# Attention and two MLPs on one core: decoding the float64 weights of the first batch in fewer, wider operations

## Chip, core and metric

The kernel runs on one NeuronCore of a Trainium2 chip. The metric is the device time of one execution in microseconds, as a median over runs.

## What is computed

A two-step attention (32 packed queries read the sequence, then the sequence reads the packed result), and two MLPs on all 4608 tokens:

```python
def sm_attn(qq, kk, vv):
    s = scale * np.matmul(qq, kk.transpose(0, 1, 3, 2))
    s = s - np.max(s, axis=-1, keepdims=True)
    a = np.exp(s)
    a = a / (np.sum(a, axis=-1, keepdims=True) + 1e-09)
    return np.matmul(a, vv)
p_packed = sm_attn(p, k, v)
out = sm_attn(q, p_packed, p_packed)
x = out.transpose(0, 2, 1, 3).reshape(4608, 512)
g = x @ w_gate
x = (g / (1 + np.exp(-g)) * (x @ w_val)) @ w_out
h = x @ w_in
return (h * np.cos(h)) @ w_out2
```

Batch 8, heads 8, sequence 576, head width 64; the first MLP has 1536 hidden columns, the second 2048. q, k, v and p are float32. The weights of both MLPs come as float64: the core reads each as two 32-bit words and makes float32 of the high word.

## The kernel before

All instructions are issued in the order in which the program is written (`tc.manual_schedule`); each engine runs its own in that order, and waits on semaphores for the others. A tile's buffer comes from a pool of a tag: `w` (24 tiles of 4 KB a partition), `c` (19), `m` (12), `s` (6), and 8 PSUM banks.

**A unit** is one decode of 512 words of a partition. `u_load` has SP load the raw words (`raw_words`, L80). `u_act` runs `decode_a` on ACT: L89 takes the high word as a float, absolute value times 65536, into `dec`, and L90 makes the low exponent bits from a byte into the result. `u_dve` runs `decode_b` on DVE: L96 raises `dec` to a least value, L97 shifts it and ors it in, L100 ors in the sign. There are 24 units for the gate and value weights (`wg`, two for each block f of 128 hidden columns) and 12 for `w_out` (`wof`, o0 to o11, three for each output block o). After a unit of `w_out`, `flush_wo` splits it: ACT copies the high half into `wo` (L77), POOL subtracts for the low half (L78); it is called in `u_dve` behind the decode of the next unit, so a split stands behind that decode. `w2_decode` uses the same decode for 256 words at a time, in batches 1 to 6.

**Stages.** Batch 0 begins with `a_s1(0)` (scores of p and k, maxima, exponentials), `a_t`, `a_pp`, `a_ppt`, `a_s2(0)` (scores of q, transposes, softmax, `af`), with first units between them (L489 to L500). Then, for every batch b:

- `a_up(b)` has 12 turns f. In batch 0 a turn makes `wp` of block f+1 (`a_wp0`: PE multiplies the packed result by `wg`, ACT copies it to `wpf`), then the gate and value products of f in four PSUM banks (L357). For each half c of the sequence ACT applies silu, the pending split of the last `h` is issued (`flush_split`: L77 on ACT, L78 on DVE), DVE multiplies `h` (L381), and `extra` issues a unit: twice a turn for f below 9, then once.
- `a_down(b)` has 8 turns n: turn n multiplies `g` with `wo` of block n // 2 (L423, 36 matmuls, three for each f; f // 4 picks the unit), and ACT evicts. `steps` holds what is issued ahead of each turn: the stages of batch b+1 (`a_s1` at 0, `a_t` at 2, `a_pp` at 3, `a_ppt` at 4, `a_s2` at 5, `a_wp` at 6), and in batch 0 two units at each of 0 to 3, one at 4, and `flush_wo` at the head of 5.

A second phase (L531 on) runs the second MLP.

Of the kernel before, what the change touches and what calls it, by code (L numbers as in the profile page):

```python
# [34 lines left out]
PASSES = ((0, 0), (0, 1), (1, 0))  # L35
LEAST = float(np.array((896 + 128) << 20, np.uint32).view(np.float32))


@with_exitstack
def attention_mlp_kernel(ctx: ExitStack, tc: tile.TileContext, qT, kT, vP, pP, wgv, w1o, w2, out):  # L40
# [92 lines left out]
    def a_s1(b):  # L133
        sp = [[bank([128, HS], "s1") for _ in range(2)] for _ in range(2)]
        for h in range(2):
            for c in range(4):
# [7 lines left out]
        for r in range(2):
# [3 lines left out]
            nm = st.tile([128, 1], F32, tag="nm", name="nm")  # L148
            DVE.tensor_scalar(out=nm, in0=mx[:, 0:1], scalar1=mx[:, 1:2], scalar2=-0.125, op0=ALU.max, op1=ALU.mult)
            e = ct([128, SPAD], F32, "E")  # L150
            nc.gpsimd.memset(e[:, S:SPAD], 0.0)
            sm = st.tile([128, 2], F32, tag="sm", name="sm")
# [5 lines left out]
            z = st.tile([128, 1], F32, tag="rs", name="rs")
            DVE.tensor_scalar(out=z, in0=sm[:, 0:1], scalar1=sm[:, 1:2], scalar2=1e-9, op0=ALU.add, op1=ALU.add)
            DVE.reciprocal(out=z, in_=z)  # L160
            E[r], rs[r] = e, z
        for j in range(NPAIR):
            del kt[b, j]
# [302 lines left out]

    with tc.manual_schedule():
        load_k(0, 0)
        load_k(0, 1)
        load_p(0)  # L470
        load_k(0, 2)
        load_k(0, 3)
        for j in range(NPAIR):
            load_v(0, j)
        u_step(0, 3)
        for j in range(NPAIR):
            load_q(0, j)
        u_step(0, 5)
        DVE.memset(zero, 0.0)
# [173 lines left out]
```

## Time and profile before

| | |
|---|---|
| median of 3 runs | 1566.46 us (1564.9 to 1567.13) |
| the profiled execution | 1567.96 us, its span 1566.2 us |
| busy PE, DVE, ACT, POOL | 1538.2 (98%), 1013.9 (65%), 713.6 (46%), 19.3 us |
| mean granted clock of TensorE | 0.992 of full speed |

The rows below come from two views. The timeline of an engine gives start and length in us, engine, line of the kernel, operation, output<-input, partitions x elements and type, how many in a row, and in brackets the idle time before with what ended it. The table of stretches gives, for each stretch of us, the busy time of each engine with its number of instructions, then the granted TensorE clock as a share of full speed (PEclk), the DMA engines' busy share and GB/s. Starts are counted from the start of the span; ends of matmuls are modelled.

### The profile page before, as it was taken

The page shows a single profiled execution, that of the slowest core. Times are in us where ns is not written, and L with a number is a line of the kernel's source. Part 1 is how long each engine was busy: PE and PEld are TensorE (multiplying, and loading weights), DVE is VectorE, ACT ScalarE, POOL GpSimd, SP SyncE. Part 2 cuts the span into 40 slices and gives each one's busy share as a digit, 9 for nine tenths or more (in the row PEclk, how much of TensorE's full clock was granted, in tenths as well). Part 3 has the DMA queues.
Part 4 walks back from the last instruction along what each step waited for, and adds up shares of the span by engine and source line. Part 5 has one row for each costly group of instructions (what it writes and reads, how often), then busy time and mean ns, then how long its engine had stood idle before and what let it go on. Part 6 is the DMA issues. An engine that isn't in the chain of part 4 may idle for free.

```text
span 1566.2 us, 24858 instructions
## 1 busy us (share of the span) xinstructions
PE 1538.2 (98%) x9796; PEld 1318.5 (84%) x9796; DVE 1013.9 (65%) x1976; ACT 713.6 (46%) x1454; POOL 19.3 (1%) x34
## 2 busy tenths in 40 slices
PE   6989999999999999999999999999999999999998
PEld 4668898989899898999978888888888888888887
DVE  6986837375583737354487676766667676776765
ACT  5874726355362635334454343333433333333333
POOL 0022000000000000000000000000000000000000
PEclk8999999999999999999999999999999999999999
DMA  8542423324151432220330101010010101010000
GB/s 305 186 146 89 146 87 125 121 78 156 46 167 59 126 119 71 89 87 5 121 94 1 54 1 54 0 55 1 12 43 1 54 0 55 0 54 1 27 1 27
DMA packets 63046, 112.25 MB, mean 72 GB/s; under 512 B 6992, under 2 KB 24656, under 8 KB 62928
## 3 DMA queue, kind: packets, MB, share of 16 engines
q1 hardware_dynamic: 53712, 101.21, 19.6%
q10 hardware_dynamic: 9216, 9.44, 1.7%
q8 instruction: 77, 1.26, 0.3%
q14 instruction: 41, 0.34, 0.1%
HBM read 83.36 MB, written 27.26 MB: 71 GB/s over the span
## 4 chain that ended last, share of the span: by engine, by line
PE 95%; DVE 3%; ACT 1%; issue 0%; DMA 0%; DVEq 0%; ACTq 0%; SPq 0%
PE acc L567 25%; PE h L540 25%; PE o L423 19%; PE pg L372 9%; PE pv L372 9%; PE wp L323 3%; PE pg L357 1%; PE pv L357 1%; PE pp L184 1%; DVE wof L100 1%; PE s L208 1%; PE wp L309 1%; PE s L138 1%; PE tp L173 0%; PE wm L482 0%; DVE wof L97 0%
## 5 line engine op out<-in xcount | busy, mean ns | idle before, releaser
L567 PE MATMUL acc<-wb,g 128*128 128x512 f32 x1728 | 416.4, 390 | 3.1 <-DVE g L78 2.5
L540 PE MATMUL h<-x,wb 128*128 128x512 f32 x1728 | 415.5, 389 | 0.0
L567 PEld LDWEIGHTS acc<-wb,g 128*128 128x128 f32 x1728 | 324.6, 188 | 71.8 <-DVE g L78 3.4
L540 PEld LDWEIGHTS h<-x,wb 128*128 128x128 f32 x1728 | 324.9, 188 | 67.6
L423 PEld LDWEIGHTS o<-g,wo 128*128 128x128 f32 x2304 | 307.3, 188 | 20.2 <-issue 10.9
L423 PE MATMUL o<-g,wo 128*128 128x288 f32 x2304 | 318.1, 297 | 4.9 <-POOL wo L78 4.1
L559 ACT ACTIVATE t<-t,half_pi 128x512 f32<-128x512 f32 x144 | 104.4, 725 | 272.6 <-DVE t L557 272.6
L552 ACT ACTIVATE t<-h,quarter 128x512 f32<-128x512 f32 x144 | 99.2, 689 | 197.8 <-PE h L540 197.7
L554 DVE TENSOR_SCALAR kk<-t 128x512 f32<-128x512 f32 x144 | 61.5, 427 | 192.4 <-ACT t L552 192.4
L372 PEld LDWEIGHTS pg<-a,wp 128*128 128x128 f32 x1008 | 142.1, 188 | 29.3 <-issue 18.4
L372 PE MATMUL pg<-a,wp 128*128 128x288 f32 x1008 | 164.9, 299 | 0.0
L372 PE MATMUL pv<-a,wp 128*128 128x288 f32 x1008 | 160.7, 294 | 0.0
L372 PEld LDWEIGHTS pv<-a,wp 128*128 128x128 f32 x1008 | 143.0, 188 | 0.0
L78 DVE TENSOR_TENSOR g<-h,g 128x288 fp32r<-128x288 f32 x192 | 87.2, 454 | 51.7 <-ACT g L77 51.7
L560 DVE TENSOR_TENSOR t<-t,h 128x512 f32<-128x512 f32 x144 | 99.1, 689 | 28.2 <-ACT t L559 28.2
L378 ACT ACTIVATE silu<-pg 128x288 f32<-128x288 f32 x192 | 78.9, 411 | 72.2 <-PE pg L372 62.2
L556 DVE SCALAR_TENSOR_TENSOR t<-kk,t 128x512 f32<-128x512 f32 x144 | 99.7, 693 | 4.9
L555 DVE SCALAR_TENSOR_TENSOR t<-kk,h 128x512 f32<-128x512 f32 x144 | 99.2, 689 | 5.0
L78 DVE TENSOR_TENSOR g<-t,g 128x512 fp32r<-128x512 f32 x144 | 98.6, 685 | 0.7 <-ACT g L77 0.7
L77 ACT ACTIVATE g<-h 128x288 fp32r<-128x288 f32 x192 | 84.5, 440 | 16.4 <-DVE h L381 15.2
L77 ACT ACTIVATE g<-t 128x512 fp32r<-128x512 f32 x144 | 89.6, 622 | 0.8 <-DVE t L560 0.8
L428 ACT ACTIVATE x2e<-o 128x288 f32<-128x288 f32 x64 | 26.2, 409 | 134.6 <-PE o L423 134.6
(82 smaller groups left out, 1128.9 us busy)
## 6 DMA issues: line engine op xcount, KB each, us to landing
raw<-in_w SPq DMA_DIRECT2D x64, 256.0 KB, 2.8
raw<-in_wgv SPq DMA_DIRECT2D x24, 512.0 KB, 7.9
vt<-in_vP SPq DMA_DIRECT2D x32, 320.0 KB, 4.6
kt<-in_kT SPq DMA_DIRECT2D x32, 288.0 KB, 4.4
qt<-in_qT SPq DMA_DIRECT2D x32, 288.0 KB, 6.2
x2d<-x2e ACTq DMA_DIRECT2D x64, 144.0 KB, 1.7
x2r<-x2d SPq DMA_DIRECT2D x36, 256.0 KB, 3.8
out<-oe SPq DMA_DIRECT2D x35, 256.0 KB, 2.0
```

The lines of the kernel that those rows point to most:

```text
L77: ACT.activation(out=hi, in_=src, func=AF.Copy)
L78: eng.tensor_tensor(out=lo, in0=src, in1=hi.bitcast(F32), op=ALU.subtract)
L372: PE.matmul(out=p_, lhsT=w[u][:, x, o:o + 128], rhs=a2[u][:, y, sl], start=(n == 0), stop=(n == 5),)
L378: ACT.activation(out=s_, in_=pg, func=AF.Silu)
L423: PE.matmul(out=acc, lhsT=wo[o, f // 4][:, x, f % 4, :], rhs=g[f][:, y, sl], start=(f == 0 and i == 0), stop=(f == NF1 - 1 and i == 2),)
L540: PE.matmul(out=p_, lhsT=wb["i", f][:, x, 128 * k:128 * k + 128], rhs=x2[t][k][:, y, :], start=(n == 0), stop=(n == 11),)
L552: ACT.activation(out=t_, in_=h_, func=AF.Identity, scale=1.0 / TWO_PI, bias=quarter)
L555: DVE.scalar_tensor_tensor(out=t_, in0=k_, scalar=-C_HI, in1=h_, op0=ALU.mult, op1=ALU.add)
L556: DVE.scalar_tensor_tensor(out=t_, in0=k_, scalar=-C_LO, in1=t_, op0=ALU.mult, op1=ALU.add)
L559: ACT.activation(out=t_, in_=t_, func=AF.Sin, bias=half_pi)
L560: DVE.tensor_tensor(out=t_, in0=t_, in1=h_, op=ALU.mult)
L567: PE.matmul(out=acc[t][i], lhsT=gt2[c][:, x, 128 * i:128 * i + 128], rhs=wb["o", f][:, y, :], start=(f == 0 and n == 0), stop=(f == NF2 - ...
```

## The change

- `decode_a`: L89 is a plain copy times 2^-112 (`REBIAS`), which keeps the sign out of the exponent's way; `decode_b` loses the operation at L96, so a decode is two DVE operations (L96 and L99 in the new numbering).
- A unit of `wg` is 1024 words, one for each f: 12 units and 12 of `w_out`. Its raw words lie in the `w` pool, whose tiles are now 8 KB and 12 in number; `wo`, and `wb` of the second phase, are kept in pairs.
- The low half of a `wo` split is a DVE subtraction. POOL keeps the memsets.
- `a_s1` issues both maxima, then all exponentials, then the reciprocals, in every batch. `a_wp0(0)` stands inside `a_s2(0)`, ahead of its softmax.
- K of batch 0 is loaded by SP (pairs 0, 1) and by ACT (2, 3).
- Batch 0 issues one unit a turn of `a_up`, at c = 0, and in `a_down` 2, 1, 2, 1, 2, 1 units at steps 0 to 5, with `flush_wo` at 6.

```diff
     def decode_a(raw, t, out):
-        ACT.activation(out=like(t, out), in_=like(raw[:, :, 1], out).bitcast(F32), func=AF.Abs, scale=65536.0)
+        ACT.activation(out=like(t, out), in_=like(raw[:, :, 1], out).bitcast(F32), func=AF.Copy, scale=REBIAS)
...
     def decode_b(raw, t, out):
         u = out.bitcast(U32)
-        DVE.tensor_scalar(out=t, in0=t, scalar1=LEAST, scalar2=None, op0=ALU.max)
...
-    units = [("g", f, i) for f in range(NF1) for i in range(2)]
+    units = [("g", f, 0) for f in range(NF1)]
...
-            split(w_, wo[a, i][:, 0].rearrange("p f o -> p (f o)"), wo[a, i][:, 1].rearrange("p f o -> p (f o)"), nc.gpsimd)
+            split(w_, wo[a, i][:, 0].rearrange("p f o -> p (f o)"), wo[a, i][:, 1].rearrange("p f o -> p (f o)"))
...
     def extra(b, f, c):
         if b == 0:
-            if f < 9 or c == 0:
+            if c == 0:
...
         load_k(0, 0)
+        load_k(0, 2, ACT)
         load_k(0, 1)
+        load_k(0, 3, ACT)
         load_p(0)
-        load_k(0, 2)
-        load_k(0, 3)
...
-        u_step(0, 3)
+        u_step(0, 2)
...
-        u_step(0, 5)
+        u_step(0, 3)
...
         a_t(0)
-        u_step(1, 2)
-        u_step(2, 2)
+        u_step(1, 1)
+        u_step(2, 1)
         a_pp(0)
         a_ppt(0)
         u_step(1, 1)
-        a_s2(0)
-        a_wp0(0)
+        a_s2(0, lambda: a_wp0(0))
         u_step(2, 1)
-        u_step(1, 3)
-        u_step(2, 3)
         u_step(1, 1)
+        u_step(2, 1)
...
-                for i in range(5):
-                    steps[i] = steps.get(i, ()) + (lambda: u_step(0, 1), lambda: u_step(1, 1), lambda: u_step(2, 1)) * (1 if i == 4 else 2)
-                steps[5] = (flush_wo,) + steps[5]
+                for i in range(6):
+                    steps[i] = steps.get(i, ()) + (lambda: u_step(0, 1), lambda: u_step(1, 1), lambda: u_step(2, 1)) * (2 - i % 2)
+                steps[6] = (flush_wo,) + steps[6]
```

Three places of the order. The first is ACT from one early turn of `a_up(0)` to the next: `raw` and `dec` belong to a unit, `g<-h` is the high half of a split. Before:

```order
L378 ACTIVATE silu_451<-pg_426 128x288
L77 ACTIVATE g_410<-h_440 128x288
L89 ACTIVATE dec_459<-raw_442 128x512
L90 ACTIVATE wg_403<-raw_442,low3_78 128x2x256
L317 ACTIVATE wpf_476<-wp_466 128x256
L317 ACTIVATE wpf_476<-wp_467 128x256
L378 ACTIVATE silu_491<-pg_479 128x288
L77 ACTIVATE g_410<-h_455 128x288
L89 ACTIVATE dec_499<-raw_457 128x512
```

Now:

```order
L389 ACTIVATE silu_453<-pg_430 128x288
L77 ACTIVATE g_414<-h_444 128x288
L328 ACTIVATE wpf_470<-wp_460 128x256
L328 ACTIVATE wpf_470<-wp_461 128x256
L389 ACTIVATE silu_485<-pg_473 128x288
L77 ACTIVATE g_414<-h_457 128x288
L89 ACTIVATE dec_494<-raw_400 128x1024
L90 ACTIVATE wg_493<-raw_400,low3_78 128x4x256
```

Between the high halves of the two `h` of a turn (`h_440` and `h_455` before, `h_444` and `h_457` now) there was half a unit, and now there is none.

The second place is DVE at such turns, where `g<-h` is the low half of a split. Before:

```order
L78 TENSOR_TENSOR g_410<-h_440,g_410 128x288
L381 TENSOR_TENSOR h_455<-silu_451,pv_427 128x288
L96 TENSOR_SCALAR dec_445<-dec_445 128x512
L97 SCALAR_TENSOR_TENSOR wg_444<-dec_445,wg_444 128x2x256
L100 SCALAR_TENSOR_TENSOR wg_444<-raw_401,wg_444 128x2x256
L78 TENSOR_TENSOR g_410<-h_455,g_410 128x288
L381 TENSOR_TENSOR h_495<-silu_491,pv_480 128x288
```

Now:

```order
L96 SCALAR_TENSOR_TENSOR wg_402<-dec_448,wg_402 128x4x256
L99 SCALAR_TENSOR_TENSOR wg_402<-raw_355,wg_402 128x4x256
L78 TENSOR_TENSOR g_414<-h_444,g_414 128x288
L392 TENSOR_TENSOR h_457<-silu_453,pv_431 128x288
L78 TENSOR_TENSOR g_414<-h_457,g_414 128x288
L392 TENSOR_TENSOR h_489<-silu_485,pv_474 128x288
L96 SCALAR_TENSOR_TENSOR wg_493<-dec_494,wg_493 128x4x256
```

Now `h_457`, the second of its turn, stands right behind a wide pair, and the next wide pair behind the `h` after it.

The third place is DVE at step 5 of `a_down(0)`, around `a_s2(1)`, whose operations are the transposes into `d1` and what follows up to the low halves of `a2`. Before:

```order
L96 TENSOR_SCALAR dec_1312<-dec_1312 128x512
L97 SCALAR_TENSOR_TENSOR wof_1311<-dec_1312,wof_1311 128x512
L100 SCALAR_TENSOR_TENSOR wof_1311<-raw_1299,wof_1311 128x512
L215 STREAM_TRANSPOSE d1_1418<-s2_1420 128x288
L215 STREAM_TRANSPOSE d1_1419<-s2_1421 128x288
L215 STREAM_TRANSPOSE d1_1418<-s2_1432 128x288
L215 STREAM_TRANSPOSE d1_1419<-s2_1433 128x288
```

Now:

```order
L236 STREAM_TRANSPOSE af_1325<-d1_1276 128x576
L78 TENSOR_TENSOR a2_1327<-af_1325,a2_1327 128x576
L96 SCALAR_TENSOR_TENSOR wof_1330<-dec_1331,wof_1330 128x512
L99 SCALAR_TENSOR_TENSOR wof_1330<-raw_1216,wof_1330 128x512
L78 TENSOR_TENSOR wo_1336<-wof_1227,wo_1336 128x512
L78 TENSOR_TENSOR wo_1336<-wof_1330,wo_1336 128x512
L78 TENSOR_TENSOR wp_1391<-wp_1381,wp_1391 128x512
```

The last unit, o11, stood ahead of `a_s2(1)` and stands behind it now, and with it the low halves of o10 (`wof_1227`) and o11 (`wof_1330`).

## Rows read from the trace of the kernel before

**Rows 1.** The table of stretches: 40 to 42 us, and the stages.

```profile
core 0: us, PE busy (x) PEld busy (x) DVE busy (x) ACT busy (x) POOL busy (x), PEclk, DMA share, GB/s
40.00:42.00 2.00, 2.00 (x6) 1.43 (x5) 1.97 (x5) 0.93 (x3) 0.00 (x0) 0.50 0.22 57
44.67:93.14 48.47, 48.47 (x306) 32.18 (x305) 46.27 (x93) 41.37 (x94) 1.27 (x1) 1.00 0.47 155
93.14:133.35 40.21, 33.30 (x266) 29.84 (x265) 29.28 (x47) 24.87 (x51) 13.97 (x12) 0.96 0.53 180
133.35:150.21 16.86, 16.86 (x157) 15.05 (x156) 12.48 (x22) 6.96 (x12) 1.30 (x1) 1.00 0.08 28
151.23:1566.20 1414.97, 1408.03 (x8832) 1219.63 (x8824) 897.21 (x1752) 616.52 (x1247) 1.84 (x12) 1.00 0.18 59
```

**Rows 2.** Timeline of PE, start and first turns of `a_up(0)`.

```profile
6.91 1.69 PE L138 MATMUL s<-kt,pt 64*32 64x288 f32 x32
...
38.39 0.86 PE L309 MATMUL wp<-wg,ppT 64*32 64x256 f32 x8 [1.14 <-DVE wg L100]
...
44.67 0.66 PE L309 MATMUL wp<-wg,ppT 64*32 64x256 f32 x16
...
49.34 0.66 PE L309 MATMUL wp<-wg,ppT 64*32 64x256 f32 x16
```

**Rows 3.** Timeline of DVE, one unit in `a_up(0)`.

```profile
57.45 0.42 DVE L96 TENSOR_SCALAR dec<-dec 128x512 f32<-128x512 f32 x1
57.91 0.69 DVE L97 SCALAR_TENSOR_TENSOR wg<-dec,wg 128x512 uint32<-128x512 uint32 x1
58.63 0.69 DVE L100 SCALAR_TENSOR_TENSOR wg<-raw,wg 128x512 uint32<-128x512 uint32 x1
59.24 0.45 DVE L78 TENSOR_TENSOR g<-h,g 128x288 fp32r<-128x288 f32 x1
```

**Rows 4.** Timeline of DVE, the last turns of `a_up(0)`.

```profile
92.28 0.45 DVE L78 TENSOR_TENSOR g<-h,g 128x288 fp32r<-128x288 f32 x1
92.65 0.44 DVE L381 TENSOR_TENSOR h<-silu,pv 128x288 f32<-128x288 f32 x1
...
95.52 1.73 DVE L100 SCALAR_TENSOR_TENSOR wof<-raw,wof 128x512 uint32<-128x512 uint32 x1
97.18 0.44 DVE L78 TENSOR_TENSOR g<-h,g 128x288 fp32r<-128x288 f32 x1
```

**Rows 5.** Timeline of ACT, the same turns.

```profile
93.13 0.44 ACT L77 ACTIVATE g<-h 128x288 fp32r<-128x288 f32 x1 [0.87 <-DVE h L381]
93.48 0.69 ACT L89 ACTIVATE dec<-raw 128x512 f32<-128x512 f32 x1
94.07 0.75 ACT L90 ACTIVATE wof<-raw,low 128x512 int32<-128x512 uint8 x1
```

**Rows 6.** Timelines of ACT and DVE, a decode of 256 words in batch 1.

```profile
152.66 0.45 ACT L89 ACTIVATE w2t<-raw 128x256 f32<-128x256 f32 x1
152.98 0.53 ACT L90 ACTIVATE w2f<-raw,low 128x256 int32<-128x256 uint8 x1
...
153.97 0.43 DVE L97 SCALAR_TENSOR_TENSOR w2f<-w2t,w2f 128x256 uint32<-128x256 uint32 x1
```

**Rows 7.** Timelines of ACT and DVE, softmax of `a_s1(0)` and end of `a_s2(0)`.

```profile
11.96 0.50 ACT L154 ACTIVATE E<-s,nm 128x288 f32<-128x288 f32 x1 [1.45 <-DVE nm L149]
...
30.21 0.78 DVE L229 STREAM_TRANSPOSE af<-d 128x576 f32<-128x576 f32 x1
```

**Rows 8.** Timeline of PE, `a_s2(1)` to the end of `a_down(0)`.

```profile
133.35 1.20 PE L208 MATMUL s<-qt,ppT 64*32 64x288 f32 x32
...
140.48 9.80 PE L423 MATMUL o<-g,wo 128*128 128x288 f32 x72
```

**Rows 9.** Timeline of DVE, the second low half of `a2`.

```profile
146.46 0.76 DVE L78 TENSOR_TENSOR a<-af,a 128x576 fp32r<-128x576 f32 x1 [0.75 <-ACT a L77]
```

More of the change, by code (lines that the diff above doesn't have):

```diff
@@ L35 @@
 PASSES = ((0, 0), (0, 1), (1, 0))
-LEAST = float(np.array((896 + 128) << 20, np.uint32).view(np.float32))
+REBIAS = 2.0 ** -112
 @with_exitstack
@@ L53, in wt @@
     def wt(shape, dt, name):
-        return sb.tile(shape, dt, tag="w", name=name, bufs=24)
+        return sb.tile(shape, dt, tag="w", name=name, bufs=12)
     def ct(shape, dt, name):
@@ L107, in load_p, with load_k @@
         SP.dma_start(out=pt[b % 2], in_=pP[b])
-    def load_k(b, j):
+    def load_k(b, j, eng=SP):
         kt[b, j] = mt([128, S], F32, "kt")
-        SP.dma_start(out=kt[b, j], in_=kT[b, j])
+        eng.dma_start(out=kt[b, j], in_=kT[b, j])
     def load_q(b, j):
@@ L143, in a_s1 @@
                     )
+        nm, sm = [], []
         for r in range(2):
@@ L147, in a_s1 @@
                 DVE.tensor_reduce(out=mx[:, h:h + 1], in_=sp[h][r], axis=AX.X, op=ALU.max)
[L148 to L152, printed above, removed]
+            nm.append(st.tile([128, 1], F32, tag="nm", name="nm"))
+            DVE.tensor_scalar(
+                out=nm[r], in0=mx[:, 0:1], scalar1=mx[:, 1:2], scalar2=-0.125, op0=ALU.max, op1=ALU.mult
+            )
+        for r in range(2):
+            E[r] = ct([128, SPAD], F32, "E")
+            nc.gpsimd.memset(E[r][:, S:SPAD], 0.0)
+            sm.append(st.tile([128, 2], F32, tag="sm", name="sm"))
             for h in range(2):
                 ACT.activation(
-                    out=e[:, HS * h:HS * h + HS], in_=sp[h][r], func=AF.Exp, scale=0.125,
-                    bias=nm, accum_out=sm[:, h:h + 1],
-                )
[L158 to L161, printed above, removed]
+                    out=E[r][:, HS * h:HS * h + HS], in_=sp[h][r], func=AF.Exp, scale=0.125,
+                    bias=nm[r], accum_out=sm[r][:, h:h + 1],
+                )
+        for r in range(2):
+            rs[r] = st.tile([128, 1], F32, tag="rs", name="rs")
+            DVE.tensor_scalar(
+                out=rs[r], in0=sm[r][:, 0:1], scalar1=sm[r][:, 1:2], scalar2=1e-9, op0=ALU.add, op1=ALU.add
+            )
+            DVE.reciprocal(out=rs[r], in_=rs[r])
         for j in range(NPAIR):
@@ L200, in a_ppt, with a_s2 @@
             ACT.activation(out=ppT[b, r], in_=tp, func=AF.Copy)
-    def a_s2(b):
+    def a_s2(b, between=None):
         d1 = [mt([128, 18, 32], F32, "d1") for _ in range(2)]
@@ L215, in a_s2 @@
                 DVE.transpose(out=d1[r][:, 9 * h:9 * h + 9, :].rearrange("p a n -> p (a n)"), in_=sp[r])
+        if between:
+            between()
         for u in range(2):
@@ L253, in u_act @@
             if a % 2 == 0:
-                wg[a // 2, i] = wt([128, 2, 2, 256], F32, "wg")
-            d_out[n] = wg[a // 2, i][:, :, a % 2, :]
+                wg[a // 2] = wt([128, 4, 2, 256], F32, "wg")
+            d_out[n] = wg[a // 2][:, :, a % 2, :]
+            d_t[n] = ct([128, 1024], F32, "dec")
         else:
             d_out[n] = mt([128, 512], F32, "wof")
-        d_t[n] = mt([128, 512], F32, "dec")
+            d_t[n] = mt([128, 512], F32, "dec")
         decode_a(d_raw[n], d_t[n], d_out[n])
@@ L275, in flush_wo @@
             a, i, w_ = wo_wait.pop(0)
-            wo[a, i] = wt([128, 2, 4, 128], F32R, "wo")
-            split(w_, wo[a, i][:, 0].rearrange("p f o -> p (f o)"), wo[a, i][:, 1].rearrange("p f o -> p (f o)"), nc.gpsimd)
+            p, e = divmod(3 * a + i, 2)
+            if e == 0:
+                wo_pair[p] = wt([128, 2, 2, 4, 128], F32R, "wo")
+            wo[a, i] = wo_pair[p][:, e]
+            split(w_, wo[a, i][:, 0].rearrange("p f o -> p (f o)"), wo[a, i][:, 1].rearrange("p f o -> p (f o)"))
     u_next = [0, 0, 0]
@@ L311, in a_wp0 @@
                     lhsT=pp_of(0, r, c),
-                    rhs=wg[f // 2, c // 2][rows(r), c % 2, f % 2, :],
+                    rhs=wg[f // 2][rows(r), c, f % 2, :],
                     start=True, stop=True,
@@ L325, in a_wp @@
                     lhsT=pp_of(b, r, c),
-                    rhs=wg[m, c // 2][rows(r), c % 2].rearrange("p a n -> p (a n)"),
+                    rhs=wg[m][rows(r), c].rearrange("p a n -> p (a n)"),
                     start=True, stop=True,
@@ L436, in attention_mlp_kernel @@
     wb = {}
-    wb_raw = {}
+    wb_raw, wb_pair = {}, {}
     def load_wb(n):
@@ L447, in split_wb @@
         r = wb_raw.pop(n)
-        wb[kind, f] = (wt if n < 24 else ct)([128, 2, 512], F32R, "wb")
+        if n < 24:
+            if n % 2 == 0:
+                wb_pair[n // 2] = wt([128, 2, 2, 512], F32R, "wb")
+            wb[kind, f] = wb_pair[n // 2][:, n % 2]
+        else:
+            wb[kind, f] = ct([128, 2, 512], F32R, "wb")
         split(r, wb[kind, f][:, 0, :], wb[kind, f][:, 1, :])
```

4 lines of the change are left out of this document (2 added, 2 removed).

## Prediction

> **What bounds the kernel now.** I read the busy time by stage first, then the timelines of PE, DVE and ACT in the first batch. From 151.23 us to the end PE is busy 1408.03 of 1414.97 us [rows 1], so what the change saves or adds elsewhere (one DVE operation less for each `w2` piece, maxima ahead of exponentials in batches 1 to 7) lies beside matmuls and is costed at nothing; without that cover it would be DVE time. The time can move only before 151 us, and a shift there reaches the end whole. Times and letters: f is a turn of `a_up(0)`, n a turn of `a_down(0)`, unit means one decode, `h(f,c)` is the gated product.
>
> The first batch has four stages. Start, to 44.67, when PE does the `wp` matmuls of f=2 [rows 2]. Then `a_up(0)`, 48.47 us, DVE busy 46.27 of them [rows 1]: PE alone could turn in 49.34 - 44.67 = 4.67 us [rows 2], but DVE needs for each half unit 1.79 us (57.45 to 59.24, three operations, [rows 3]) plus the low half of a split and an `h` of 0.37 us each [rows 4], twice per f: 2 x (1.79 + 0.74) = 5.06 us. Then `a_down(0)` to the scores of batch 1, 40.21 us with PE busy 33.30, so 6.9 us of pauses, and the last three turns, 16.86 us without one [rows 1].
>
> **Price of a wide operation.** No 1024-word operation is in the trace. L97 on 256 words takes 0.43, on 512 0.69; L89 0.45 and 0.69; L90 0.53 and 0.75 [rows 3, 5, 6]. The same step twice more gives 1.21, 1.17 and 1.19 us. Start to start: L97 to L100 is 0.72 and L100 to the next 0.61 on 512 words [rows 3], so 1.24 and 1.13 on 1024, a pair of 2.37; L89 to L90 0.59 [rows 5], so 1.07. If a word cost a tenth more or less, the whole unit, 1.07 + 1.19 + 2.37 = 4.63 us, moves by 0.46.
>
> **Start.** The second `E` waits 1.45 us for a maximum that now comes earlier [rows 7]. That moves the softmax chain up by at most 1.45; the first `raw` is twice as long and a half unit no longer overlaps the other half, so I take 1.0 (ends 0.3 and 1.45). The last `af` of `a_s2(0)` ends at 30.21 + 0.78 = 30.99 [rows 7], now about 30.0. Until PE gets the `wg` of f=1 DVE then has two pairs, 4.74 us, to 34.7, where PE now waits until 38.39 [rows 2]. Unit 3 starts on ACT at about that time and takes 4.63, to 39.3, and PE's `wp` of f=2 needs it: 39.4 against 44.67. The clock is granted at 0.50 in 40 to 42 [rows 1], the lower of its levels, 1.2 of 2.4 GHz, after those waits, so f=1 takes 6.28 (38.39 to 44.67); this is inside the difference. I take **-5.0 us** (-4 to -6). The second K queue I cost at nothing: L138 starts at 6.91 with no idle before it, PE being filled by its warm-up matmuls [rows 2]. The earlier `wpf` copies let f=0 start earlier, but f=1 waits for unit 2 anyhow. The larger `raw` tiles move Q behind half a megabyte more on SP; that is within the ends of the first 1.0.
>
> **`a_up(0)`.** DVE's own need falls to 2.37 + 4 x 0.37 = 3.85 us per f, under PE's 4.67. But the order closes a ring. With one unit per f, at c=0, `h(f,1)` stands on DVE behind the unit's pair; ACT's high half of `h(f,1)` waits for it; ACT's Copy for the next unit stands behind that high half; and DVE's pair waits for ACT. Before, the unit at c=1 gave ACT work ahead of that wait. The ring can be seen at the end of `a_up(0)`, where the old program too has one unit per f: low half at 92.28, `h` at 92.65 [rows 4], high half at 93.13, L89 at 93.48, L90 at 94.07 [rows 5], L100 at 95.52, low half again at 97.18 [rows 4]: 4.90 us, of which L100 has 1.66 instead of 0.61 beside POOL's subtraction; without it 3.85. With wide operations it is 0.37 + 0.48 + 0.35 + 1.07 + 1.19 + 1.24 + 1.13 = 5.83 us. PE's `wp` at f needs the unit of f-2, so PE takes that pace: from f=2 to f=10 8 x 5.83 = 46.6, then 4.67 and about 4.0 for the two turns that need no new unit: 55.3 against 48.47, **+6.8 us** (a tenth of the unit either way: +3.1 to +10.5).
>
> The operations of [rows 3] follow each other on DVE without a gap, and the wide pair does cost DVE less: 2.37 against 2 x 1.79 = 3.58. The Trainium skill (Perfetto Trace Analysis, Optimizing Scalar/DVE Operations) says of this both that larger operations can raise throughput where the engine is saturated, and that breaking instructions up may finish work sooner where Scalar or Vector is not saturated but causes bubbles elsewhere. By the first alone the stage would run at 4.67 and the term be -2.4; the second goes with the +6.8 above, and the ring of [rows 4, 5] is on its side.
>
> **`a_down(0)`, n=0 to 4.** The split's subtraction moves from POOL to DVE. A unit there costs DVE 0.72 + 0.61 + 0.61 = 1.94, before 1.79, or 2.83 where POOL stretched L100 to 1.73 [rows 3, 4]. So DVE gets freer, but PE now waits for the high half on ACT and then a low half that stands behind the next unit's pair. The pauses change owner; I take **+1.0 us** (-6.9, all pauses gone, to +3, 1 us more at each of n=0, 2 and 4).
>
> **`a_down(0)`, n=5 to 7.** Before, the decoding is over and `flush_wo` empty before step 5. Now step 5 issues `a_s2(1)` first and the last unit (o11) behind it, and o10's split is flushed only after o11's decode. Let S be the start of the scores (133.35, [rows 8]). PE reaches n=6 at S + 7.13 (140.48) and, at 9.80 / 72 = 0.136 us a matmul, its thirteenth matmul, the first to need o10, at S + 8.76. ACT is through the high half of the second `a2` when DVE starts its low half, S + 13.11 (146.46, [rows 9]); then come L89 and L90 (0.59 + 0.75), to S + 14.45, DVE's pair (0.72 + 0.61), and the low half of o10, 0.69 like any pass over 512 words [rows 3], to S + 16.5. Two matmuls need the high half alone, 0.27. Stall: 16.5 - 8.76 - 0.27 = 7.4 us. After it the clock should be low as at 40 us: f=1 lost 6.28 - 4.67 = 1.6 there. Together **+9.0 us** (0 if nothing is late, to +10).
>
> **Sum.** -5.0 + 6.8 + 1.0 + 9.0 = +11.8 on the profiled execution's 1567.96, 1579.8; the median is 1.5 lower, so 1578.3. Its own range by the ends is 1573 to 1584.
>
> **Rivals.**
> - DVE was what was short, and its relief counts everywhere: 4.67 per f (-2.4), the 6.9 us of pauses gone, the last stall of 9.0 left: -5.0 - 2.4 - 6.9 + 9.0 = -5.3, 1561.2, faster. It is decided at one point: whether L89 of the next unit starts before `h(f,1)` is done on DVE. For it: DVE's 46.27 of 48.47 [rows 1]. Against: ACT's order, and [rows 4, 5]. Chance 0.07. This is what the first sentence of that section of the Trainium skill would lead to.
> - Ring, but no stall at n=6, o10 and o11 being ready in time: -5.0 + 6.8 + 1.0 = +2.8, 1569.3. Against it DVE's order around `a_s2(1)`. 0.06.
> - Stall, but no ring: -5.0 - 2.4 + 1.0 + 9.0 = +2.6, 1569.1. 0.07.
> - Wide words cost a tenth more (strided `raw`, four pieces of 256): the ring is 6.29, +10.5 instead of +6.8, 1582.0. 0.08.
> - The forecast: 0.72.
>
> **Numbers.** A measurement here tells about 0.2%, 3.1 us, from no change. The second and third rival lie just inside it; I count 0.11 as same and 0.02 as slower. Faster 0.07, same 0.11, slower 0.82. The range 1571 to 1584 holds the forecast's own ends and the fourth rival and leaves the first three out, 0.20.
>
> **What would show it.** Right: wide L89, L90, L96 and L99 near 1.17, 1.19, 1.21 and 1.21 us; `wp` of f=2 near 39.4 and then every 5.8 us; DVE idle over 1 us before each wide L96, released by ACT, and ACT idle before the high half of `h(f,1)`; one PE pause of 6 to 7 us in n=6 with a low clock behind it; batch 1 starting some 12 us after 151.23. Wrong: `wp` turns near 4.7, or no pause in n=6; a gap after batch 1 would mean that the rest is not covered by PE.

## The result and the profile after

The changed kernel takes 1575.84 us (median of six runs, 1575.22 to 1577.9) against 1566.8 us before (six runs beside them, 1564.9 to 1567.79): a ratio of 1.0062, interval 1.0049 to 1.0075. It is slower by 9.0 us, and inside the range; the forecast was 1578.3. The profiled execution took 1575.22 us, its span is 1573.2.

The table of stretches of the changed kernel, cut at the same events as [rows 1]: `wp` of f=2, scores of `a_s1(1)`, scores of `a_s2(1)` and the `wp` that `a_up(1)` starts with, called `wp` of batch 1's second turn in the texts below (for the last row, that `wp` is over).

```profile
core 0: us, PE busy (x) PEld busy (x) DVE busy (x) ACT busy (x) POOL busy (x), PEclk, DMA share, GB/s
0.00:39.76 39.76, 25.76 (x232) 19.08 (x232) 23.39 (x44) 19.96 (x38) 0.88 (x8) 0.91 0.97 385
39.76:95.43 55.67, 46.51 (x305) 31.51 (x305) 38.67 (x63) 39.01 (x79) 0.30 (x2) 1.00 0.27 94
95.43:132.76 37.33, 31.39 (x266) 28.15 (x265) 23.01 (x46) 24.04 (x50) 0.00 (x0) 1.00 0.53 182
132.76:159.04 26.28, 19.75 (x158) 17.37 (x157) 15.41 (x27) 8.67 (x15) 0.00 (x0) 0.87 0.08 27
160.06:1573.20 1413.14, 1406.39 (x8832) 1218.45 (x8824) 879.20 (x1688) 615.20 (x1247) 1.83 (x12) 1.00 0.18 60
```

In the second row DVE has less to do than before (38.67 against 46.27 us, [rows 1]), and yet the stage is 7.2 us longer. No engine of that row is busy throughout; the busiest is PE, with 46.51 of 55.67 us. A ring can look like this in such a table: every engine has idle time, and the stage is longer than any one's work. The stages give -4.9 (start), +7.2, -2.9 and +9.4: +8.8.

The timeline of PE of the changed kernel shows the two places (columns as in [rows 2]).

```profile
35.09 0.67 PE L320 MATMUL wp<-wg,ppT 64*32 64x256 f32 x16 [1.24 <-DVE wg L99]
...
39.76 0.66 PE L320 MATMUL wp<-wg,ppT 64*32 64x256 f32 x16
...
45.62 0.67 PE L320 MATMUL wp<-wg,ppT 64*32 64x256 f32 x16 [1.11 <-DVE wg L99]
...
51.51 0.67 PE L320 MATMUL wp<-wg,ppT 64*32 64x256 f32 x16 [1.15 <-DVE wg L99]
...
132.76 1.20 PE L213 MATMUL s<-qt,ppT 64*32 64x288 f32 x32
...
139.90 1.85 PE L434 MATMUL o<-g,wo 128*128 128x288 f32 x12
147.60 0.85 PE L434 MATMUL o<-g,wo 128*128 128x288 f32 x2 [5.85 <-ACT wo L77]
149.13 9.98 PE L434 MATMUL o<-g,wo 128*128 128x288 f32 x58 [0.69 <-DVE wo L78]
```

A turn of `a_up(0)` takes 5.89 us (45.62 to 51.51), and each `wp` from 45.62 on waits for the last operation of a unit, L99. One such turn, timeline of DVE, changed kernel:

```profile
45.76 0.45 DVE L392 TENSOR_TENSOR h<-silu,pv 128x288 f32<-128x288 f32 x1
46.71 0.46 DVE L78 TENSOR_TENSOR g<-h,g 128x288 fp32r<-128x288 f32 x1 [0.51 <-ACT g L77]
47.09 0.45 DVE L392 TENSOR_TENSOR h<-silu,pv 128x288 f32<-128x288 f32 x1
48.88 1.22 DVE L96 SCALAR_TENSOR_TENSOR wg<-dec,wg 128x1024 uint32<-128x1024 uint32 x1 [1.34 <-ACT wg L90]
50.14 1.22 DVE L99 SCALAR_TENSOR_TENSOR wg<-raw,wg 128x1024 uint32<-128x1024 uint32 x1
51.28 0.45 DVE L78 TENSOR_TENSOR g<-h,g 128x288 fp32r<-128x288 f32 x1
```

The same turn, timeline of ACT:

```profile
46.24 0.44 ACT L77 ACTIVATE g<-h 128x288 fp32r<-128x288 f32 x1 [1.81 <-DVE h L392]
46.59 1.15 ACT L89 ACTIVATE dec<-raw 128x1024 f32<-128x1024 f32 x1
47.64 1.21 ACT L90 ACTIVATE wg<-raw,low 128x1024 int32<-128x1024 uint8 x1
```

Read them as one loop: `h` at 45.76 lets ACT go at 46.24; L89 and L90 follow; DVE has waited 1.34 us for L90 when it starts L96 at 48.88; L99, a low half (51.28) and the next `h` close it. ACT waits 1.81 us a turn for DVE, DVE 1.85 us for ACT.

At the end of `a_down(0)`, timeline of ACT, changed kernel:

```profile
145.15 0.68 ACT L77 ACTIVATE a<-af 128x576 fp32r<-128x576 f32 x1 [3.60 <-DVE af L236]
145.74 0.65 ACT L89 ACTIVATE dec<-raw 128x512 f32<-128x512 f32 x1
146.29 0.74 ACT L90 ACTIVATE wof<-raw,low 128x512 int32<-128x512 uint8 x1
146.94 0.61 ACT L77 ACTIVATE wo<-wof 128x512 fp32r<-128x512 f32 x1
```

And of DVE:

```profile
147.06 0.69 DVE L96 SCALAR_TENSOR_TENSOR wof<-dec,wof 128x512 uint32<-128x512 uint32 x1 [0.44 <-ACT wof L90]
147.78 0.69 DVE L99 SCALAR_TENSOR_TENSOR wof<-raw,wof 128x512 uint32<-128x512 uint32 x1
148.39 1.47 DVE L78 TENSOR_TENSOR wo<-wof,wo 128x512 fp32r<-128x512 f32 x2
```

The split of o10 (146.94, 148.39) waits behind `a2` and the whole decode of o11. PE stands for 6.54 us, and then the clock is at its lower level (stretches of 2 us, changed kernel, columns as above):

```profile
144.00:146.00 2.00, 0.00 (x0) 0.00 (x0) 1.22 (x3) 0.85 (x2) 0.00 (x0) 1.00 0.00 0
146.00:148.00 2.00, 0.40 (x1) 0.40 (x2) 1.53 (x3) 1.84 (x4) 0.00 (x0) 0.70 0.00 0
148.00:150.00 2.00, 1.31 (x5) 0.97 (x5) 1.91 (x4) 1.49 (x3) 0.00 (x0) 0.50 0.21 74
150.00:152.00 2.00, 2.00 (x10) 2.00 (x10) 1.06 (x2) 0.11 (x1) 0.00 (x0) 0.50 0.00 0
```

The granted clock falls from 1.00 to 0.50 during the pause, and PE, busy throughout 150 to 152, starts 10 matmuls there, where 2 us at 1.00 hold 17 (e12_flush_ahead, 144 to 146). So the stage is 9.4 us longer although the pause is 6.5: some 2.9 us are the clock's.

### The profile page after: what moved, and what is told of

Its sections match the earlier page's. It is cut to its first block, busy times and chain, and to the rows that moved or that the text cites. A ratio compares the mean times of both kernels' runs of the same rounds, so it can differ in the third digit from the quotient of the medians.

```text
span 1573.2 us, 24618 instructions
## 1 busy us (share of the span) xinstructions
PE 1530.8 (97%) x9796; PEld 1314.7 (84%) x9796; DVE 979.7 (62%) x1864; ACT 707.3 (45%) x1430; POOL 3.0 (0%) x22
## 4 chain that ended last, share of the span: by engine, by line
PE 92%; DVE 4%; ACT 3%; issue 1%; ACTq 0%; DVEq 0%
PE acc L581 25%; PE h L554 25%; PE o L434 18%; PE pg L383 9%; PE pv L383 8%; PE wp L334 3%; PE pp L189 1%; ACT dec L89 1%; DVE wg L96 1%; ACT wg L90 1%; DVE wg L99 1%; PE s L137 1%; PE s L213 1%; PE pg L368 0%; PE wm L498 0%
```

## The experiments

Twelve kernels. Lengths of the stages in us, from the timelines of PE, cut as above; "median" is of the runs, the ratio is to the runs of the kernel before beside them (medians of before: 1567.37 beside e1 to e4, 1566.56 beside e5 to e8, 1565.98 beside e9 to e11, 1567.35 beside e12).

| kernel | to `wp` f=2 | `a_up(0)` | n=0..4 | n=5..7 | median | ratio (95% interval) |
|---|---|---|---|---|---|---|
| before | 44.67 | 48.47 | 40.21 | 16.86 | 1566.8 | |
| changed | 39.76 | 55.67 | 37.33 | 26.28 | 1575.84 | 1.0062 (1.0049, 1.0075) |
| e1_ring | 39.73 | 47.07 | 38.33 | 26.61 | 1569.43 | 1.0019 (1.0007, 1.0032) |
| e2_tail | 40.71 | 55.70 | 37.37 | 16.87 | 1566.92 | 1.0009 (1.0000, 1.0019) |
| e3_both | 40.88 | 47.01 | 36.77 | 16.88 | 1558.73 | 0.9957 (0.9944, 0.9971) |
| e4_half | 38.58 | 45.91 | 33.58 | 25.22 | 1562.46 | 0.9978 (0.9969, 0.9988) |
| e5_half_tail | 39.45 | 45.90 | 34.06 | 16.88 | 1554.12 | 0.9914 (0.9899, 0.9929) |
| e6_two_ops | 40.74 | 45.91 | 36.77 | 16.88 | 1558.75 | 0.9943 (0.9928, 0.9958) |
| e7_dve_split | 43.49 | 48.91 | 37.09 | 16.88 | 1565.16 | 0.9993 (0.9984, 1.0003) |
| e8_maxima | 41.71 | 48.91 | 37.03 | 16.87 | 1563.48 | 0.9975 (0.9964, 0.9986) |
| e9_unit_ahead | 39.90 | 55.71 | 37.33 | 26.09 | 1575.26 | 1.0064 (1.0048, 1.0081) |
| e10_one_queue | 41.10 | 55.65 | 39.73 | 26.77 | 1577.95 | 1.0073 (1.0056, 1.0090) |
| e11_v_earlier | 38.54 | 46.06 | 35.98 | 16.86 | 1553.1 | 0.9919 (0.9904, 0.9935) |
| e12_flush_ahead | 39.65 | 55.59 | 37.34 | 16.89 | 1569.65 | 1.0019 (1.0010, 1.0029) |

### Opening the ring: e1_ring

The changed kernel; in batch 0 a unit is asked of ACT right behind the silu of c=0, ahead of the high half that waits for DVE.

```diff
                 ACT.activation(out=s_, in_=pg, func=AF.Silu)
+                if b == 0 and c == 0:
+                    u_step(0, 1)
+                    u_step(1, 1)
                 flush_split()
...
             if c == 0:
-                u_step(0, 1)
-                u_step(1, 1)
                 u_step(2, 1)
```

> The changed kernel, with ACT's two operations of a unit issued ahead of the pending high half in the turns of a_up(0); everything else, the late last unit too, as changed. If the ring is what sets the turns, wp comes every 4.7 to 4.9 us instead of 5.89, a_up(0) from f=2 on takes about 46.5 instead of 55.67 us, the pause in n=6 stays at 6 to 7 us, and the time is about 1567 us. If wide operations as such are too slow for the stage, or the raw words come late, the turns stay near 5.9 and the time at 1576.

`a_up(0)` fell from 55.67 to 47.07 us with every operation as wide as before, and nothing was taken off any engine. Timeline of DVE of this kernel:

```profile
56.09 0.45 DVE L395 TENSOR_TENSOR h<-silu,pv 128x288 f32<-128x288 f32 x1
56.45 1.22 DVE L96 SCALAR_TENSOR_TENSOR wg<-dec,wg 128x1024 uint32<-128x1024 uint32 x1
57.70 1.23 DVE L99 SCALAR_TENSOR_TENSOR wg<-raw,wg 128x1024 uint32<-128x1024 uint32 x1
```

L96 now follows `h` without the 1.34 us of waiting. So the 5.89 us a turn were order, not work. The pause in n=6 (5.87 + 0.69 us) stayed, as it should. The median is 2.4 us over the 1567 named: the stage is 0.6 us longer than the 46.5 named, and n=0 to 4 is 1.0 us longer than in the changed kernel, at a granted clock of 0.96 there.

### The last unit: e2_tail, and both: e3_both

e2_tail is the changed kernel with the units spread over `a_down(0)` as before; e3_both has the edits of e1_ring and e2_tail.

```diff
-                for i in range(6):
-                    steps[i] = steps.get(i, ()) + (lambda: u_step(0, 1), lambda: u_step(1, 1), lambda: u_step(2, 1)) * (2 - i % 2)
-                steps[6] = (flush_wo,) + steps[6]
+                for i in range(5):
+                    steps[i] = steps.get(i, ()) + (lambda: u_step(0, 1), lambda: u_step(1, 1), lambda: u_step(2, 1)) * (1 if i == 4 else 2)
+                steps[5] = (flush_wo,) + steps[5]
```

> The changed kernel, with the units of a_down(0) at 2, 2, 2, 2, 1 in steps 0 to 4 and the flush at the head of step 5, as before the change. If DVE's order around a_s2(1) makes the pause in n=6, the pause is gone, n=5 to 7 take 17 instead of 26.28 us, the clock stays up there, and the time is about 1567 us; the turns of a_up(0) stay at 5.89. If o10 and o11 are late because their raw words or DVE are late in any order, PE waits as long at n=4 or n=5 instead and the time stays at 1576.

> Both edits of the two runs before this one. If ring and late unit are separate terms their gains add: turns near 4.7 to 4.9, no pause in n=6, about 1558 us, 0.5% below the kernel before. If the gain of one is given back at the other (PE only waits later, for V or for the units of a_down), about 1565.

In e2_tail the last stage is 16.87 us again, the clock stays up, and the turns of `a_up(0)` keep their 5.89 us; in e3_both the turns are 4.8 us as well. So the two costs are separate. Against the changed kernel's 9.0 us over before, e1_ring stands at +2.1, e2_tail at -0.5 and e3_both at -8.6: 7.0, 9.5 and 17.7 us off, so both together gain 1.2 us more than the sum of the two. The ratios don't rest on the medians alone and put e2_tail 1.4 us over before; by them the three gains are 6.7, 8.3 and 16.4 us.

The spread of the units also decides what PE waits for in n=0 to 4. PE's waits in that stage, before and then in the changed kernel (waits: engine line waited for, us in total, times, longest):

```profile
PE o L423 <- POOL wo L78: 4.1, 5, 1.0
PE pp L184 <- DMA vt<-in_vP: 2.0, 2, 1.4
PE o L423 <- ACT wo L77: 0.7, 1, 0.7
```

```profile
PE o L434 <- DVE wo L78: 4.8, 6, 1.0
PE o L434 <- ACT wo L77: 1.1, 3, 0.7
```

Before, 4.8 us of waits are for halves of `wo` and 2.0 for V of batch 1 (`vt`); in the changed kernel 5.9 and none. Three pairs differ in the spread alone: changed and e2_tail, e1_ring and e3_both, e4_half and e5_half_tail. In each the old spread has waits for V (1.8 to 2.4 us) where the new one has none, and 1.9 to 2.8 us less of waits for `wo`; the two nearly cancel.

### Half-wide units: e4_half and e5_half_tail

e4_half is the changed kernel with units of 512 words, two a turn up to f=8, and with the first units issued as in the kernel before; e5_half_tail adds the edit of e2_tail.

```diff
-    units = [("g", f, 0) for f in range(NF1)]
+    units = [("g", f, i) for f in range(NF1) for i in range(2)]
...
-            if c == 0:
+            if f < 9 or c == 0:
...
-        u_step(1, 1)
-        u_step(2, 1)
+        u_step(1, 2)
+        u_step(2, 2)
...
+        u_step(1, 3)
+        u_step(2, 3)
         u_step(1, 1)
-        u_step(2, 1)
```

> The changed kernel with units of 512 words again, two a turn (at c=0 and c=1), loaded and started as before the change; two-operation decode, DVE for the split, the order of a_s1, the K queues and the late last unit as changed. If the ring needs one unit a turn standing behind the high half, it is open here: turns of 4.67 to 4.8 (DVE needs about 4.2), the start some 0.5 us later than the changed one, the pause in n=6 stays, about 1567 us. If the turns are slow for the amount of decoding or the new pools, they stay near 5.9 and the time at 1576.

> The changed program with units of 512 words (two a turn of a_up(0)) and with the old distribution of the units over the steps of a_down(0) (2, 2, 2, 2, 1 at steps 0 to 4, flush_wo at step 5). Theory (of the change's parts only the width of the units, through the ring, and the last unit behind a_s2(1) cost time): a_up(0) keeps the pace of e4_half, 4.67 us a turn; the scores of a_s2(1) start near 118 to 120 (118.07 in e4_half, up to 2 us later where V lands late, as in e2_tail and e3_both); from there 16.9 us without a pause, so wp of batch 1's second turn at 135 to 137 against 143.29; median 1555 (1553 to 1557). Rival (the pauses of 4.72 + 1.36 us only move to turns 0 to 4 when two units stand at each step, as the old program had 6.9 us there): s2 at 124, 1560 to 1561.

The turns are 4.67 us, PE's own pace. I had not expected the third stage to shrink as well, to 33.58 and 34.06 us, which puts e4_half 4.5 us under the 1567 named. PE's waits there for the halves of `wo` are 5.9 us in the changed kernel, 2.6 in e4_half and 0.7 in e5_half_tail. What DVE waited for points to a reason: from 84 us on in the changed kernel, then from 74 us on in e5_half_tail (columns of waits as above).

```profile
DVE wof L96 <- ACT wof L90: 9.8, 7, 5.2
```

```profile
DVE wo L78 <- ACT wo L77: 7.4, 4, 3.3
```

In the changed kernel DVE waits seven times for ACT's half of the very unit it is to finish; in e5_half_tail never. A likely reason lies in the first units (`u_step(1, k)` issues ACT's half of k units, `u_step(2, k)` DVE's): the kernel before and e4_half issue seven ACT halves and six DVE halves ahead of the loop, so ACT is always a unit ahead; the changed kernel issues three and three. The change took away not only half a unit between two high halves but that lead, and e4_half gives both back. The lead alone doesn't make 34 us: e6_two_ops to e8_maxima below have it too, take 36.8 to 37.1 us for the stage, and have 2.6 to 2.8 us of waits for `wo` in it. So the reason for the shorter third stage is argued, not shown. Wide units with a unit's lead weren't tried, so how much of the 13.4 us between the changed kernel and e4_half is width and how much the lead stays open; e1_ring shows that the width needn't cost much of it. e5_half_tail, 12.4 us faster than before, beats both kernels.

### What each good part is worth: e6_two_ops, e7_dve_split, e8_maxima

Each is the kernel before with one part of the change.

```diff
-        ACT.activation(out=like(t, out), in_=like(raw[:, :, 1], out).bitcast(F32), func=AF.Abs, scale=65536.0)
+        ACT.activation(out=like(t, out), in_=like(raw[:, :, 1], out).bitcast(F32), func=AF.Copy, scale=REBIAS)
...
-        DVE.tensor_scalar(out=t, in0=t, scalar1=LEAST, scalar2=None, op0=ALU.max)
```

> The kernel before, with one part of the change alone: the decode in two DVE operations (no raising to a least value). Theory (at 512 words a unit it is DVE's time that is short, so that the relief counts): DVE's need for a turn of a_up(0) falls from 2 x 2.53 = 5.06 to 2 x 2.07 = 4.14 us, under PE's 4.67, so the stage takes about 46 instead of 48.5 us; four half units ahead of the second turn save up to 4 x 0.46 = 1.8 us of the start; median 1562 to 1563.5. Rival (what bounds the stage is the order between ACT and DVE at this width too, DVE's busy share being a symptom): stage and median as before, 1566 to 1567.5.

7.8 us faster, more than expected: the start gains 3.9 and `a_up(0)` 2.6, now at PE's pace with PE busy all 45.91 us of it, and n=0 to 4 gains 3.4, which I had left out (9.9 in all between the two profiles, of which the one before stood 1.2 over its median).

e7_dve_split only takes `nc.gpsimd` out of the call of `split` in `flush_wo`.

> The kernel before, with one part of the change alone: the low halves of wo are subtracted by DVE instead of POOL. Theory (POOL's subtraction stretches the DVE operation beside it from 0.69 to 1.7 us, so a subtraction of 0.61 on DVE itself is no dearer): all L100 near 0.69, the pauses of a_down(0)'s turns 0 to 4 (6.9 us before) fall by 0 to 3 us, median 1564 to 1567. Rival (DVE is the engine that is short there, and one operation more for each of 12 units costs its 0.61 us): 7 us more DVE work, up to 4 of it seen, 1568 to 1571.

1.4 us faster by the medians, with an interval that holds no change. The groups of instructions up to 165 us in e7_dve_split and, below, in e8_maxima, where POOL still subtracts (busy time, mean ns of one, idle time before):

```profile
L100 DVE SCALAR_TENSOR_TENSOR wof<-raw,wof 128x512 uint32<-128x512 uint32 x12 | 8.3, 692 | 0.4
L78 DVE TENSOR_TENSOR wo<-wof,wo 128x512 fp32r<-128x512 f32 x12 | 8.2, 687 | 3.9 <-ACT wo L77 3.8
```

```profile
L78 POOL TENSOR_TENSOR wo<-wof,wo 128x512 fp32r<-128x512 f32 x12 | 16.5, 1373 | 112.5 <-ACT wo L77 112.5
L100 DVE SCALAR_TENSOR_TENSOR wof<-raw,wof 128x512 uint32<-128x512 uint32 x12 | 15.2, 1266 | 0.4
```

With POOL's subtractions beside it L100 takes 1266 ns in the mean instead of 692, 6.9 us of DVE time over 12 units; the twelve subtractions on DVE cost 8.2. So DVE's time is hardly changed, and POOL's 16.5 us are gone. The Trainium skill (SBUF — State Buffer, Who interferes with whom) has it that a DVE operation with two SBUF inputs and a GpSimd operation reading SBUF exclude each other for whole instructions; the trace agrees: in the profile before, the L100 of [rows 4] (1.73 us) ends 0.54 us behind the POOL subtraction beside it (95.43 to 96.71), and an L100 with none beside it takes 0.69.

In e8_maxima `a_s1` has the text of the changed kernel.

> The kernel before, with one part of the change alone: all maxima ahead of the exponentials in every a_s1. Theory (it moves the softmax of batch 0 up by at most 1.45 us, and of that only what DVE doesn't lose again behind two decodes reaches PE; the other batches are covered): 1565.5 to 1567.3, no difference that can be told. Rival (the start is one chain from the maxima to wp of the second turn): 1.0 to 1.45 us earlier there and 1565.5 or less.

3.1 us faster; neither expectation was that large. The two waits of `tp` for `E` before (1.57 and 1.49 us) are one of 1.63, which gives the 1.4 expected; the further 1.5 us to `wp` of f=2 are the turn of f=1, 6.28 us at the lower clock before and 4.64 here. It is 4.65 in e7_dve_split too, whose `a_s1` is unchanged, so the maxima don't make it. How much of the median's 3.1 us is clock stays open. The three parts add up to 12.3 us, and e5_half_tail, which has them all and neither of the two costs, gained 12.4. That is a sum of medians; in the single profiles the stages don't add up so well (starts 3.9, 1.2 and 3.0 us earlier, against 5.2), so part of the agreement may be chance.

### Where the last split stands: e9_unit_ahead, e12_flush_ahead

In the changed kernel, step 5 only: e9_unit_ahead issues the unit ahead of `a_s2(1)` and keeps `flush_wo` at step 6; e12_flush_ahead issues `flush_wo` there as well (the edit below).

```diff
-                    steps[i] = steps.get(i, ()) + (lambda: u_step(0, 1), lambda: u_step(1, 1), lambda: u_step(2, 1)) * (2 - i % 2)
-                steps[6] = (flush_wo,) + steps[6]
+                    us = (lambda: u_step(0, 1), lambda: u_step(1, 1), lambda: u_step(2, 1)) * (2 - i % 2)
+                    steps[i] = us + (flush_wo,) + steps.get(i, ()) if i == 5 else steps.get(i, ()) + us
```

> The changed program; only within step 5 of a_down(0) the order is turned: the unit o11 (and with it the split of o10) is issued ahead of a_s2(1); flush_wo, which splits o11, stays at step 6, behind a_s2(1). Theory (what makes the pause is the place in the order of ACT and DVE): o10 is no longer waited for; o11's split now stands where o10's stood, without a decode ahead of it: high half about S + 13, low half about S + 14.6 (S the start of the scores); PE wants o11 twelve matmuls or 1.63 us after o10, at S + 10.4. So the pause in turn 6 shrinks from 5.85 + 0.69 to 3 to 4.5 us and lies twelve matmuls later, the low clock behind it stays; median 1572 to 1574. Rival (o10 and o11 are late because their words or DVE's time come late, whatever the order): the pause stays in front of o10's matmuls with over 5 us, 1575 to 1577.

A miss for both sides. Timelines of PE and of ACT, e9_unit_ahead:

```profile
140.08 3.44 PE L434 MATMUL o<-g,wo 128*128 128x288 f32 x24
150.77 8.33 PE L434 MATMUL o<-g,wo 128*128 128x288 f32 x48 [7.25 <-ACT wo L77]
```

```profile
148.71 0.68 ACT L77 ACTIVATE a<-af 128x576 fp32r<-128x576 f32 x1 [3.61 <-DVE af L236]
149.29 0.39 ACT L439 ACTIVATE x2e<-o 128x288 f32<-128x288 f32 x1
149.72 0.33 ACTq L440 DMA_DIRECT2D x2d<-x2e  x1
150.09 0.63 ACT L77 ACTIVATE wo<-wof 128x512 fp32r<-128x512 f32 x1 [0.40 <-ACT x2e L439]
```

The median is in the rival's range, but the pause isn't where the rival has it. It moved twelve matmuls on (24 before it instead of 12), from o10 to o11, as the theory said, but it did not shrink: 7.25 us and 1575.26 us. The sum had left out what the moved unit costs `a_s2(1)`, whose second high half comes at 148.71 instead of 145.15, and the eviction and its DMA issue, 149.29 and 149.72, that stand ahead of o11's high half.

> As e9_unit_ahead, and flush_wo too stands ahead of a_s2(1) in step 5: the unit o11 and both splits lie before the scores' chain on ACT and DVE, the number of units at each step is as in the changed program. Theory (what PE waits for in turn 6 is whatever split stands behind a_s2(1)): no pause in turn 6 and no low clock after it; a_s2(1)'s chain comes some 3 us later on DVE as in e9_unit_ahead (first transpose at S + 4.2), which PE doesn't wait for before batch 1, 16.9 us after S; wp of batch 1's second turn near 150 instead of 159.04; median 1566 to 1568.5. Rival (the later chain is seen: PE waits for a2 of batch 1 at its start): a pause of 1 to 3 us in front of batch 1's first gate products, 1568.5 to 1571.

With the flush ahead too, the pause and the low clock are gone (16.89 us, PE busy all of it). The rival is seen as well; batch 1 starts with this (timeline of PE, e12_flush_ahead):

```profile
151.19 0.53 PE L383 MATMUL pg<-a,wp 128*128 128x288 f32 x2 [0.63 <-ACT wp L77]
151.91 1.00 PE L383 MATMUL pg<-a,wp 128*128 128x288 f32 x4 [0.20 <-DVE wp L78]
```

The median is 6.2 us under the changed kernel's, in the rival's range, where e2_tail is 8.9 under it. The two profiles, which lie near their medians, tell where that goes. At `wp` of batch 1's second turn e12_flush_ahead is 1.2 us ahead (149.47 against 150.65). Its first turns of batch 1, with the 0.83 us of waits above, cost it 1.4 us, and the second phase 2.8: there the clock fell behind two short waits that both kernels have, and ten matmuls took 4.63 us instead of 2.57 (last section). So in these profiles the time lies in the rival's range more through the clock than through the rival's pause. What PE waited for in turn 6 was each time the split that stood behind `a_s2(1)`; that is shown by the three kernels together.

### Two smaller questions: e10_one_queue, e11_v_earlier

e10_one_queue is the changed kernel with the four loads of K on SP; e11_v_earlier is e5_half_tail with `load_v` and `load_q` of batch 1 at turn 1 of `a_down(0)`.

> The changed program with K of batch 0 loaded by SP alone, as before. Theory (the scores wait for the warm-up matmuls and not for K): s starts right behind wm, the stages as in the changed program, 1575 to 1577. Rival (the second queue brings the start of the scores forward): s has a pause for kt in front of it, 0.3 to 2 us, 1576.5 to 1578.

The scores start at 7.06 us, with no wait for `kt`, right behind the warm-up, as the theory has it; the median lies in the rival's range all the same. 1577.95 us is 2.1 over the changed kernel, but the intervals overlap, and in the profile most of the difference lies in stretches of low clock (0.91 instead of 1.00 in n=0 to 4: 39.73 against 37.33 us, for the same instructions). No worth of the second queue is shown.

> e5_half_tail with V of batch 1 (and its Q) asked for at turn 1 of a_down(0) instead of turn 2. Theory (V is the last of PE's waits there, 0.77 + 0.29 + 0.69 us, because SP reaches its loads late): the waits for vt at pp go, 0.5 to 1.7 us less, 1552.5 to 1554. Rival (SP waits for buffers that decoded words give free, so V comes no sooner, or the words behind it in SP's queue come later and PE waits for wo instead): 1554 to 1556.

The waits for `vt` (1.8 us in e5_half_tail) are gone, and `ppt` waits 2.79 us for `ppu` instead. `ppu` stands on DVE behind a low half of `wo`, which waited 5.07 us for ACT's high half; and ACT waited for raw words of `w_out` (waits of ACT, e11_v_earlier):

```profile
ACT dec L89 <- DMA raw<-in_w1o: 5.3, 1, 5.3
```

e5_half_tail has no such wait. So V came sooner and words came later, the second half of the rival; in the profile that cost PE more than it gained. 1553.1 against 1554.12 us can't be told apart.

## Why the prediction was right

- **Start, forecast -5.0, measured -4.9.** `wp` of f=2 at 39.76, forecast 39.4. On the way the last `af` ended at 30.18, forecast 30.0, and `wp` of f=1 came at 35.09, forecast 34.7; from there PE, no longer at its lower clock, took 4.67. Unit 3, which the forecast waited for, was done on DVE at 39.59 (39.3 reckoned), 0.2 us before PE came to it, so PE's pace and the unit bound alike. Not reckoned were a start of the scores 1.1 us later (8.01 against 6.91), behind a longer warm-up, and a faster `pp` (2.40 us against 4.47). PE then waited 3.36 us for `ppu` instead of 0.86, so that of both only 0.8 us is left at `ppt` (18.44 against 19.24), near the 1.0 that was forecast for the chain.
- **`a_up(0)`, forecast +6.8, measured +7.2.** Turns of 5.89 us against 5.83. The wide operations were 1.15, 1.21, 1.22 and 1.22 us where 1.17, 1.19, 1.21 and 1.21 were reckoned from 256 and 512 words: within 2%. The ring of [rows 4, 5] was the right thing to read, and e1_ring showed it. Rival 1, that DVE's relief counts everywhere, fell at the point named for it: L89 starts at 46.59, after `h`. But it was true of the turns of the half-wide program (e6_two_ops, 4.67 us), though not of the pauses behind them, of which 5.0 us were left. Of the two sentences of the Trainium skill (Perfetto Trace Analysis, Optimizing Scalar/DVE Operations) the one on breaking up goes with the changed kernel; still, e3_both is 8.6 us faster than before with the large operations kept, so the order decided, and width alone did not.
- **n=0 to 4, forecast +1.0, measured -2.9: mis-sized.** PE's waits for the halves of `wo` grew by 1.1 us (4.8 to 5.9), with DVE and ACT as their owners, as the forecast had it. What it left out is the rest of the stage. The 2.0 us of waits for V are gone, which goes with the new spread of the units (e2_tail, e3_both). And PE's busy time is 31.39 against 33.30 us [rows 1]: the granted clock, 0.96 in that row, was 0.50 from 121 to 123 us in the profile before, right behind the waits for V, and is 1.00 all through the stage here. I took 40.21 for the stage's length before, and read neither the waits for V nor the 0.96 in it. The same stage with any one part of the change alone is 36.8 to 37.1, and e10_one_queue, with the changed kernel's order, took 39.73 at a clock of 0.91: through the clock alone this term moves by 2 us from one execution to the next.
- **n=5 to 7, forecast +9.0, measured +9.4.** The low half of o10 let PE go at 149.13, 16.4 us after the scores' start, forecast 16.5; the pause was 6.5 us instead of 7.4, as PE came 0.2 us later to o10 and its first two matmuls, at the lower clock, took 0.85 us instead of 0.27; the low clock cost 2.9 instead of 1.6. That the sum is so near is luck in part: the two misses have opposite signs.
- **The rest, forecast 0.** No gap after batch 1. The last stretch is 1.8 us shorter, 1.6 of it PE's busy time (1406.39 against 1408.03), which is the clock (last section). That profile is a favourable execution: its mean granted clock is 0.996, that of the other five runs 0.991 or 0.992, and they are 0.4 to 2.7 us longer.

Sum of the stages +8.8 against +11.8, and the median 2.5 us under the forecast: the third term missed by 3.9 us, the others by 0.1 to 0.4 the other way. The forecast's "own range by the ends", 1573 to 1584, isn't what the ends of its four terms add up to; those run from -9.8 to +19.5, or from 1556.7 to 1586. The range that was stated is thus tighter than the working behind it.

## What to carry over

When a profile shows one engine nearly full, ask before shortening its work whether the order in which two engines hand work to each other would close a ring. The sign is two engines that wait for each other once a turn. Here the ring opened when one engine's half was issued a step ahead, with every operation as wide (e1_ring); half-wide units with their lead of a unit opened it too (e4_half), but there width and lead were changed together. Fewer operations did pay where the order was kept (e6_two_ops, 7.8 us). And when the last items of a spread-out job are placed behind a long dependent chain, reckon from that chain's end when they come, with every eviction and DMA issue that stands between, and with what the moved work adds to the chain itself (e9_unit_ahead was missed for want of these).

## What was not expected of the hardware

**The clock after equal pauses.** At the passage to the second phase PE waits 0.60 and then 1.90 us in every profile, at 782 us before and at 791 after; then, from the stretches of before and of the changed kernel:

```profile
786.00:788.00 2.00, 2.00 (x7) 1.57 (x6) 1.93 (x5) 1.05 (x2) 0.00 (x0) 0.55 0.15 11
```

```profile
795.00:797.00 2.00, 2.00 (x11) 1.65 (x10) 1.93 (x5) 0.86 (x2) 0.00 (x0) 1.00 0.27 32
```

The granted clock fell to about half in one and stayed at 1.00 in the other, for the same pauses; 7 matmuls start in 2 us or 11. Of the fourteen profiles the clock fell there in eight (before, e3 to e7, e11 and e12) and stayed up in six. From the end of the first wait to the end of the span the eight take 783.8 to 785.1 us, and five of the six 782.2 to 782.4. The sixth, e1_ring, takes 784.1 for another reason: its matmuls are over as soon as the changed kernel's, 778.6 us after that wait, but 5.4 us pass from there to the end instead of 3.6. What decides the clock was not tried.

**The clock of the start.** The 36 warm-up matmuls took 5.93 us in the profile before and 7.03 after, and the 40 `pp` matmuls 4.47 and then 2.40; over the other profiles the two mostly go against each other (5.71 with 3.65, 6.90 with 2.40, but 6.58 with 3.24). A profile's first 20 us are not to be compared to better than a microsecond.
